# A smaller leading tile for the first convolution of a speech joint network, with its weight sums on other operands and engines

## The chip, the cores and the metric

One core of a Trainium2 chip. The metric is the device time of one execution in microseconds (us), as the median of several runs. Engines: TensorE (PE; its weight loads are the row PEld), VectorE (DVE), ScalarE (ACT), GpSimd (POOL) and SyncE (SP), which issues nearly all DMAs.

## The reference

Two strided convolutions over time, then a joint network. All tensors are bf16.

```python
B, T, D, K, U = 2, 4000, 512, 5, 8
h = sum over i of einsum("btc,cd->btd", xp[:, i:i+T, :], w1[i])      # xp: x padded by 2 at both ends
h = gelu(h)[:, ::2, :]                                              # 2000 rows per batch element
f = sum over i of einsum("btc,cd->btd", hp[:, i:i+T1, :], w2[i])
f = gelu(f)[:, ::2, :]                                              # 1000 rows
fe = einsum("btd,de->bte", f, w_f);  ge = einsum("bud,de->bue", g, w_g)
j = tanh(fe[:, :, None, :] + ge[:, None, :, :])
out = einsum("btud,dv->btuv", j, w_o)                               # 2 x 1000 x 8 x 512
```

## The kernel before, in words

**Tiles.** Channels stand on the 128 partitions, in four blocks of 128; time runs along the free dimension. The first convolution (conv1) of batch element 0 is cut into three tiles: a leading one of 2 x `NA` = 408 outputs, and two later ones with `N3` = 266 columns each, which give 3 x 266 = 798 outputs each (L311). Batch element 1 is two tiles of 334 columns, and the second convolution (conv2) two tiles of 334.

**The leading tile** is computed plainly. Its rows of x are loaded as they stand (`load_xr`, two loads of 128 and 78 rows of four time steps), turned on TensorE against an identity (`turn`, L489), and copied from PSUM into `xs`. Then `direct` (L691) runs 80 matmuls, 5 taps by 4 by 4 blocks, in the order of taps 0, 4, 2, 1, 3, each with 408 moving columns, into four PSUM banks.

**A later tile** (`Triple`, L562, and `Unit`, L607) computes three neighbouring outputs together from nine products, each on sums and differences of inputs and of weights. Its inputs come by transposing DMAs, one for each of six phases of time (`xq`, `load_xq`, L464). The sums of inputs are made in 17 `STEPS` (L773): "d" copies a doubled phase, "r" and the rest subtract or add, "next" and "prev" copy a shifted phase. A product is 16 matmuls (4 by 4 blocks), a tile 9 x 16 = 144. For each output block, `Unit` runs five steps with copies out of PSUM between them: `s1` keeps 1.5 times the first product ("c"), `s2` keeps minus the next ("s"), `s3` to `s5` finish the three outputs.

**The sums of conv1's weights** (`w1part`, L542) are made on the chip, block by block of 128 output channels (m = 0 to 3), on 512 elements per partition: t = w0 + w4, u = 4 w4 + w0, u = 2 w2 + u, v = t - w2, and t + w2, all on VectorE in SBUF; ScalarE then writes u/3 and v/3 as bf16 into `w1_x`. w1 + w3, w1 - w3 and 2 w1 are made for two blocks at a time. The first products of a later tile need u/3 of all four blocks and the first difference of x.

**The order.** Every operation is recorded with its reads and writes (`Plan`, L110). `ORDER`, a table of characters at the head of the file, holds for each engine the list of recorded operations in the order in which it runs them. The kernel holds the finished table, not what made it. `schedule` (L199) reads it; `flex` (L130) records an operation that can run on either of two engines, and the table then says on which. `emit` places the waits that the order leaves needed. So an engine never passes over an operation that waits.

**PSUM.** Banks 0 to 3 hold the leading tile; banks 4 to 7 and then 3 go to the units of the later tiles.

**After the convolutions** the features and the joint output are computed by fast (seven-product) block multiplications, whose sums are on VectorE or GpSimd, tanh on ScalarE, evictions on ScalarE and VectorE, and stores on SyncE's queue.

Of the kernel before, what the change touches and what calls it, by code (L numbers as in the profile page):

```python
# [12 lines left out]
P = 128  # L13
# [50 lines left out]
class Op:  # L64
# [6 lines left out]
        "0Y0Z0a0b0c0d0e0f0g0i0k0l0n0q0y0z0_0-101112131415161718191A1B1C1D1E1F1G1H1p2L2l321I1J2v2S2T1r1s2w2n2N2o2O34352y2V2z2W"  # L71
        "3F3G3C3D392s3X2t3A3Y3Q3S3g3T403a3b3q4A3n3i3r3j3d4J423e4T4B434U3o473t4L4j4M4D3u484E4h4W4Q4k4R5U4X4u4r4x4s4o524z4p4_4v"
        "5e55565y535f586667595W5X5b5c6U5_6W5h6e6X5-6f6u6h6i6364695i6-726b6c6w6A736x707H7a7J7K7y7R7k7O7l7S7h7U7P757V7i7c867d7_"
        "7-767n8c8C897o8A8M87838N8J848e8K8f8E8F8v8_8w8m8n989990918j8P958k8Q9B8x8y9M9O8p9P8q9T9U969Z9a9c9C9o9x9d9W9z9X9qA5ACA2"
        "ABA4A99sAWAGAI9tArAsANAKB3B4BAAiAQAjATBBARAUBMAlAmBeBNAoApBfBtAyAzBGBhBiA-BTBUB0BDBHBEBJCABzBaBKBbBWBXCBBkBlCQCHB_CI"
        "CNBnC0COC1BqBoCKBrCLCuCcC6CdCRCfCvCgCTCjCkC7CxCyCUDODSDBDCDTC_DeDEC-DFCnCoD1DVD2DWDfDYDKDZDlDoDLDpDmDwE1E2D4E4E5D5Db"
        "DcDxDsDtENE7E8EOEKEDEEEiEAEjEBELEcEXEYEdF7ETEoFLEUF0EfElFMEgF1F8FXEmFDFOFfF3FBFPFgFsF4F_G4F-FRFiG5FZFjFSFUFVG1G2GNGG"
        "GHGTGUFoFpFuGAGWG7G8GZGXGJGKGOGaGnGoGcGqGrGhGfHCGwGxH0GdHEH3H1HVH4H9HWHAHbHhH6I4I5HKHNHcHLH7HOHjHpHqHeHYHZHfHRHSIAI7"
        "I8IKHyHzHsIhIbIBILHtIcIiIDJ4J5INIOIRIeISIEIkJKIrIsIfJAJBIlJLJDI_J7IuIvJXI-J8JdJaJbJYJEJgJeJRJNJhK0K1JnJoJSJqJwJOKGK6"
        "JrK3K4KHKbJxK7KVKWK9KcKAKYKZL0KeKfKlKmKNL1KOKJKuL6KKKoL7LZKpL3LTL9KvLGLULaLHLALcL4LyLNLsLjLOLkLtLzLdLJLKLWM2LXM3MCMR"  # L80
        "L-M0MSMuMDMvLmLnM5MJM6MhMiMKMFMUMXMGMVMYMaMxMyMbM_N1M-NPN8N9MoMkNQMpN2MlNBNCNFNGNSNTNYNuNvO1ONNZOONfNgNiNjNVNWN_O2Nx"
        "NyN-O8OdNmOeNnO9OwOTOWOUOxOqOrOXOBOQOCOtOROFOkOuOGP4OzP5OgPBPCOlOhP7O_PHPIPKP8PLPiQ9PjPQPRPNPOQAPXPYPaPrPoPpPbPsPlPm"
        "PyPePfPzQMP-Q0Q3Q4QNQCQDQIQJQFQGQPQQQTQUQXQYQbQeQfQi"),
    "act": (
        "080h0m1U0r1x1W1a1z1Z251Y2b1q271K2m1L2M1-1j2U1t2x1l1M1O332d2R1N3E2g2f2X2u2_3Z3B3H3R2h3h413c2r3K3s3M4K3x3f4C4V3p3y3w38"
        "494F4b3m3W3v4i5V5D464t4Y4P4S4y4d5C574q4w5z5B4n6E5A5g5154685d6V6g786j6v6G6M6a5j65795S6B5a745T627I7A7b6d7s5x7z7T717N6_"
        "7W7j7m5q6T7Q5w778D8d7u7g828O8B886s6t7p6S8X8-8L858o8Y9A8W9G8I8R8i8l9N7G948r9I976m9b9V9D9e9S8z9p9_9rA69YAcAXA8AFAtAdAP"
        "AfAMAeAhASAnBOAVB8BuB9AgBgCFCECs9wB7CGCqB-CJC2CCCrCDCeCwChDQCtDPDRFJDDD-CpE0DGDgEaDnFHCXEbE3D6FxFFFGFID_FwEMEFEZEPGS"
        "FyEpFNF2FYFKG_FCF5FhFzIWFkG-GIGVFvI0IVJ2GpGRGgGsHDJVH2J_HXI2IYHMHPI6I1IXIaJ-IMICIjJ6IdJ3ItI3IZJMIwJWJZK_JfK2JpKTJsNN"
        "KILSKdKRK-KnL2KUKyKqLwL8LVLILRLlL_NqKSLxM4MTMEMwMtMjMHKzMQNsN0MPMmNDNLNRMsOPNhNwNXNkNtNMOfOMNOODNrOpP6OLOiPJOoP9PPPZ"  # L90
        "PkQBPcPqP_Q1QOQHQRQgQdQk"),
    "dve": (
        "000j0o0p1R1S1v1T1V1X231w1u212Z1_1y24221b2a261d1c1Q1e1g1f1P1h1i1k28202p1m2P2Y362c1n2Q2q372e1o302i2k2j2-3U3I3V313J3L3k"
# [191 lines left out]
def bass_standalone__seq2seq_rnn_t_joint__speech_kernel(  # L285
# [35 lines left out]
    with ExitStack() as es:  # L321
# [142 lines left out]
        def load_xq(i, ph):  # L464
            o = load_x6(xq[i], 0, ph, 2 * NA // 3 + i * N3[0] - 2, 0, -(-(N3[i] + 3 - i) // 16) * 16)
            if (i, ph) in ((0, 4), (0, 0)):
                o.wire = 1.050 if ph else 2.520
# [768 lines left out]
```

## Time and profile before

| what | value |
|---|---|
| runs | 248.55, 249.01, 249.67 us (median 249.01) |
| profiled execution, first to last instruction (span) | 247.2 us |
| TensorE busy | 242.8 us, 98% |
| VectorE busy | 224.8 us, 91% |
| ScalarE busy | 210.7 us, 85% |
| GpSimd busy | 83.8 us, 34% |

The profile gives the span of its execution; the execution's own total time is not listed beside it, so the median of the runs stands for it, 1.8 us above the span. The profile's page has busy times, 40 slices of the span, the chain that ended last, and groups of instructions by line of the kernel. Other views of the same trace list instructions in order of time, by tile, by stage and by wait. A row of the view in order of time reads: start, length from first start to last end, engine, line, operation, what it writes and reads with sizes, count, and the idle time ahead of it with what ended it. Neighbouring instructions on an engine overlap a little, so distances between starts, not lengths, add up to a queue's time.

### The profile page before, as it was taken

What the parts mean: (1) busy time and instruction counts of PE and PEld (TensorE: products, weight loads), DVE (VectorE), ACT (ScalarE), POOL (GpSimd) and SP (SyncE); (2) the same over time, 40 slices, a digit from 0 to 9 for tenths busy, and PEclk for the clock granted to TensorE, in tenths of its full rate; (3) what the DMA queues carried; (4) which work ended last, traced back from release to release, by engine and by line L of the source; (5) the groups of instructions that cost most, each with busy time, mean ns of one, the idle gap of its engine ahead of it and who ended that gap; (6) DMA issues with size and microseconds to landing.
All of it is one profiled execution on the core that took longest, in us unless ns stands there. A gap on an engine that the chain in (4) does not pass through costs nothing.

```text
span 247.2 us, 5277 instructions
## 1 busy us (share of the span) xinstructions
PE 242.8 (98%) x1932; PEld 186.1 (75%) x1932; DVE 224.8 (91%) x403; ACT 210.7 (85%) x359; POOL 83.8 (34%) x90
## 2 busy tenths in 40 slices
PE   8999999999999999999999999999999999999995
PEld 4657888877666666666567888778788888888883
DVE  1799998867999999699998999999999999999994
ACT  3269799899669857986799999999999999999992
POOL 1000000000000000000015584677887886796861
PEclk9999999999999999999999999999999999999999
DMA  6998999997700340000000234413433655356377
GB/s 215 331 193 168 185 157 205 150 177 174 254 2 3 119 135 3 1 1 3 0 0 3 85 102 139 143 48 129 131 127 103 195 171 172 132 187 200 123 258 233
DMA packets 57890, 31.87 MB, mean 129 GB/s; under 512 B 33835, under 2 KB 57659, under 8 KB 57865
## 3 DMA queue, kind: packets, MB, share of 16 engines
q1 hardware_dynamic: 57577, 31.41, 48.5%
q8 instruction: 15, 0.25, 0.4%
q10 hardware_dynamic: 288, 0.13, 0.2%
q14 instruction: 10, 0.08, 0.1%
HBM read 7.66 MB, written 16.38 MB: 97 GB/s over the span
## 4 chain that ended last, share of the span: by engine, by line
PE 98%; DVE 0%; issue 0%
PE acc L412 97%; PE acc L496 1%; DVE ost L835 0%; DVE xs L505 0%; DVE zero L419 0%
## 5 line engine op out<-in xcount | busy, mean ns | idle before, releaser
L398 DVE TENSOR_TENSOR og<-acc,sn 128x512 bf16<-128x512 f32 x93 | 60.0, 690 | 1.9 <-PE acc L412 1.2
L412 PE MATMUL acc<-tw,ss 128*128 128x256 f16 x372 | 58.0, 273 | 0.0
L404 ACT ACTIVATE jT<-feT,geT 128x1000 bf16<-128x1000 f32 (+6 forms) x56 | 53.2, 1002 | 1.8 <-DVE feT L398 1.5
L834 ACT ACTIVATE sn<-acc 128x512 f32<-128x512 f32 (+1 forms) x70 | 43.0, 707 | 1.0 <-PE acc L412 0.7
L412 PEld LDWEIGHTS acc<-tw,ss 128*128 128x128 f16 x372 | 36.0, 98 | 6.5 <-ACT sn L834 0.2
L903 POOL TENSOR_TENSOR ss<-jT 128x512 f16<-128x512 bf16 x24 | 27.7, 1168 | 25.0 <-DVE feT L398 22.5
L412 PE MATMUL acc<-row,w_sb 128*128 128x334 bf16 (+1 forms) x192 | 31.7, 296 | 0.0
L412 PE MATMUL acc<-wo_sb,jT 128*128 128x256 bf16 x176 | 29.2, 273 | 0.0
L404 ACT ACTIVATE sd<-acc 128x334 f32<-128x334 f32 (+1 forms) x48 | 20.6, 435 | 10.1 <-PE acc L412 9.6
L412 PE MATMUL acc<-row,w_x 128*128 128x266 bf16 (+1 forms) x192 | 28.4, 291 | 0.0
L404 ACT ACTIVATE jX<-feT,geT 128x1000 bf16<-128x1000 f32 (+4 forms) x28 | 27.4, 1042 | 0.0
L394 POOL MEMSET hT<- 128x8 bf16 (+2 forms) x6 | 0.7, 149 | 70.5 <-ACT hT L404 70.5
L412 PEld LDWEIGHTS acc<-row,w_sb 128*128 128x128 bf16 x192 | 18.7, 98 | 6.3
L412 PEld LDWEIGHTS acc<-row,w_x 128*128 128x128 bf16 x192 | 18.7, 98 | 5.7
L903 POOL TENSOR_TENSOR ss<-jT,ss 128x512 f16<-128x512 bf16 x14 | 16.6, 1189 | 15.1 <-DVE ss L903 9.7
L412 PE MATMUL acc<-wo_sb,ss 128*128 128x256 bf16 x124 | 21.0, 273 | 0.0
L412 PEld LDWEIGHTS acc<-wo_sb,jT 128*128 128x128 bf16 x176 | 17.2, 98 | 3.1
L835 DVE COPY sn<-acc 128x512 f32<-128x512 f32 (+1 forms) x25 | 16.8, 691 | 1.1 <-PE acc L412 1.0
L412 PE MATMUL acc<-hT,w_sb 128*128 128x334 bf16 x96 | 17.1, 305 | 0.0
L518 DVE SCALAR_TENSOR_TENSOR acc<-acc,sd 128x334 f32<-128x334 f32 (+1 forms) x24 | 11.7, 487 | 5.8 <-PE acc L412 5.6
L404 ACT ACTIVATE hT<-acc 128x266 bf16<-128x266 f32 (+2 forms) x36 | 14.6, 433 | 2.7 <-PE acc L412 2.4
L834 ACT ACTIVATE og<-acc 128x512 bf16<-128x512 f32 x22 | 15.3, 710 | 1.5 <-PE acc L412 1.5
(113 smaller groups left out, 502.5 us busy)
## 6 DMA issues: line engine op xcount, KB each, us to landing
out_dram<-og SPq DMA_DIRECT2D x45, 256.0 KB, 2.3
w_sb<-in_w_dram SPq DMA_DIRECT2D x8, 512.0 KB, 4.9
out_dram<-og SPq DMA_DIRECT2D x19, 128.0 KB, 2.2
w_sb<-in_w_dram SPq DMA_DIRECT2D x4, 256.0 KB, 4.8
xr<-in_x_dram SPq DMA_DIRECT2D x1, 512.0 KB, 3.5
wf_sb<-in_w_f_dram SPq DMA_DIRECT2D x1, 512.0 KB, 3.6
wg_sb<-in_w_g_dram SPq DMA_DIRECT2D x1, 512.0 KB, 5.1
wo_sb<-in_w_o_dram SPq DMA_DIRECT2D x1, 512.0 KB, 5.2
```

The lines of the kernel that those rows point to most:

```text
L394: pl.op("pool", lambda e: e.memset(v.ap, 0.0), (), (v,))
L398: pl.op(eng, lambda e: e.tensor_tensor(out=o.ap, in0=a.ap, in1=b.ap, op=op), (a, b), (o,), 0.02 + 2.14e-3 * o.ap.free_size() if eng == "po ...
L404: pl.op("act", lambda e: e.activation(o.ap, i.ap, func, scale=scale, bias=0.0 if bias is None else bias.ap), rd, (o,), o.ap.free_size() * ...
L412: ins = e.matmul(o.ap, lhsT=l.ap, rhs=r.ap, start=start and n == 0, stop=stop and n == len(pairs) - 1, skip_group_check=not check)
L496: ins = e.transpose(pv.ap[:, i, k, :], xr[rt].h[0:n, 2 * r + pp, k, :], ident.h[0:n, 0:n])
L518: pl.op(eng, lambda e: e.scalar_tensor_tensor(out=o.ap, in0=a.ap, scalar=f, in1=b.ap, op0=ALU.mult, op1=add), (a, b), (o,), vec_cost(o, (a ...
L834: pl.flex({"act": (lambda e: e.activation(o.ap, v.ap, ACT.Copy), 0.05 + n * 0.833e-3), "dve": (lambda e: e.tensor_copy(out=o.ap, in_=v.ap) ...
L835: "dve": (lambda e: e.tensor_copy(out=o.ap, in_=v.ap), 0.065 + n * 1.04e-3)}, (v,), (o,))
L903: fn = lambda e, o=S[i], x=x, y=y, op=op: e.tensor_tensor(out=o.ap, in0=x.ap, in1=y.ap, op=op)
```

## The change

The leading tile goes from 408 to 360 outputs and the two later ones from 266 and 266 to 234 and 314 columns; the buffers of the transposed loads grow with it.

```diff
-        NA, N3 = 204, (266, 266)
+        NA, N3 = 180, (234, 314)
-        xq = [Buf(nc, f"xq{i}", [6, NK, (288, 288)[i]], BF16, v.end - v.bytes) ...]
+        xq = [Buf(nc, f"xq{i}", [6, NK, (352, 352)[i]], BF16, v.end - v.bytes) ...]
```

The loads of taps 1 and 3 are gated by an earlier arrival: tap 3 waits for the first half of tap 4 instead of the second.

```diff
-                              (4, (slice(0, NK), slice(D // 2, D)), 0), (2, None, 1), (1, None, 3), (3, None, 5)):
+                              (4, (slice(0, NK), slice(D // 2, D)), 0), (2, None, 1)):
             load_w1(i, part, gate)
-        for ph in (4, 0, 2, 1, 3, 5):
-            load_xq(0, ph)
+        for kind, i in (('w', 1), ('w', 3), ('x', 4), ('x', 0), ('x', 2), ('x', 1), ('x', 3), ('x', 5)):
+            if kind == "w":
+                load_w1(i, None, len(came) - 4)
+            else:
+                load_xq(0, i)
```

The weight sums: for every block, ScalarE first copies tap 4 into a PSUM bank (of banks 4 to 7), and u is built there. For blocks 0 and 1 ("P") t and v are in PSUM too, on VectorE. For blocks 2 and 3 ("G") GpSimd makes t, v and t + w2 in SBUF. The sums of taps 1 and 3 may run on either engine.

```diff
+        WBANK = ((6, 7), (5, 4), (6, 7), (5, 4))
+        WHOME = ('P', 'P', 'G', 'G')
...
+            home = WHOME[m]
+            if home != "S":
+                u, t = (ps.cols(bk * NT, NT).map(lambda a: a.rearrange("p (k c) -> p k c", k=NK)) for bk in WBANK[m])
+                act(u, w(4), ACT.Copy)
+                w4 = u
...
+            if home == "G":
+                t, v = ssum[4][:], ssum[m % 2][:]
+                tt("pool", t, w(0), w(4), add)
+                tt("pool", v, t, w(2), sub)
+                tt("pool", w1_t[2, :, sl], t, w(2), add)
+            else:
+                v = t if home == "P" else ssum[m % 2][:]
+                tt("dve", t, w4, w(0), add)
+            stt("dve", u, w4, 4.0, w(0))
+            stt("dve", u, w(2), 2.0, u)
+            act(w1_x[1, :, sl], u, ACT.Copy, scale=1.0 / 3.0)
+            if home != "G":
+                tt("dve", w1_t[2, :, sl], t, w(2), add)
                 tt("dve", v, t, w(2), sub)
+            act(w1_x[0, :, sl], v, ACT.Copy, scale=1.0 / 3.0)
+
+        def w13part(m):
+            n = slice(m * P, (m + 2) * P)
+            shared(w1_x[2, :, n], w1_sb[1, :, n], w1_sb[3, :, n], sub, True)
+            shared(w1_t[0, :, n], w1_sb[1, :, n], w1_sb[3, :, n], add, True)
+            scaled(w1_t[1, :, n], w1_sb[1, :, n], 2.0)
```

The scaled copies of `Triple` and `Unit` (steps "d", "next", "prev", and "c" and "s") go through `scaled`, which lets the table put them on ScalarE or VectorE.

```diff
+        def scaled(o, i, f):
+            n = o.ap.free_size()
+            fast = not i.psum and o.ap.dtype == BF16 and i.ap.dtype == BF16
+            pl.port = fast
+            pl.flex({"act": (lambda e: e.activation(o.ap, i.ap, ACT.Copy, scale=f), n * 0.833e-3 + (0.05 if i.psum else 0.105)),
+                     "dve": (lambda e: e.tensor_scalar_mul(out=o.ap, in0=i.ap, scalar1=f), 0.065 + n * (0.26e-3 if fast else 1.04e-3))}, (i,), (o,))
+            pl.port = False
...
-                    act(r(i, n=E), z(2 * i - 2, 0, E) if i else z(4, -1, E), ACT.Copy, scale=2.0)
+                    scaled(r(i, n=E), z(2 * i - 2, 0, E) if i else z(4, -1, E), 2.0)
...
-                act(self.c, self.pa(), ACT.Copy, scale=1.5)
+                scaled(self.c, self.pa(), 1.5)
```

The zeroed edges of the second tile's input are written phase by phase (six small writes on GpSimd, not two). The planner's figures for the turns change (0.275 to 0.43, 0.2 to 0.19), and the whole `ORDER` table is replaced: every engine's order is new, from the start of conv1 to the last store. In it ScalarE's second copy of turned rows comes before the weight sums, 18 of the scaled copies are on VectorE, GpSimd has 77 of the two-operand sums of the later stages instead of 71, and at the end the product for the last two-operand eviction stands behind the first half of the last plain tile, not ahead of it.

More of the change, by code (lines that the diff above doesn't have):

```diff
@@ L780, in steps @@
             when(slot, *[lambda w=w: trip[i].step(w) for w in STEPS[lo:hi]])
-        w1part(0, "s")
+        for m in range(NK):
+            w1part(m, "s")
+        for m in (0, 2):
+            w13part(m)
         for w in STEPS:
             trip[0].step(w)
-        for m in range(1, NK):
-            when((0, 0, 1)[m - 1], lambda m=m: w1part(m, "s"))
         when(17, load_late, lambda: tail_zero(1))
```

108 lines of the change are left out of this document (48 added, 60 removed).

## The prediction

> **What bounds the kernel now.** I read the page first, then the chain that ended last, the waits of TensorE, and the opening 30 us engine by engine.
>
> ```profile
> PE 242.8 (98%) x1932; PEld 186.1 (75%) x1932; DVE 224.8 (91%) x403; ACT 210.7 (85%) x359; POOL 83.8 (34%) x90
> PE   8999999999999999999999999999999999999995
> PEclk9999999999999999999999999999999999999999
> ```
>
> TensorE is busy in every slice at a full granted clock. The chain that ended last (start, length, what) and the waits of TensorE agree:
>
> ```profile
> 4.78 2.18 PE acc L496 x24
> 6.96 0.02 issue
> 6.99 0.33 DVE xs L505
> 7.32 0.05 issue
> 7.37 236.76 PE acc L412 x1892
> ...
> 244.15 0.42 DVE ost L835
> ```
> ```profile
> PE acc L412 <- DVE zero L419: 1.2, 1, 1.2
> ```
>
> From 7.37 to 244.15 us the chain never leaves TensorE, and its only listed wait is the one before its first instruction. So the time is an opening of 7.37 us, a stream of matmuls without gaps, and a tail. Only the columns streamed, the opening and the tail can shorten it; any wait added between lengthens it. A busy TensorE could hide small gaps, so I look at the starts:
>
> ```profile
> 4.58 2.66 PE L496 MATMUL acc<-ident,xr 128*128 128x128 bf16 x32
> 7.37 12.65 PE L412 MATMUL acc<-xs,w_sb 128*128 128x408 bf16 x72
> 19.86 1.98 PE L412 MATMUL acc<-row,w_x 128*128 128x266 bf16 x16
> 21.67 1.54 PE L412 MATMUL acc<-xs,w_sb 128*128 128x408 bf16 x8
> ```
>
> Start to start, a 408-column matmul takes (19.86 - 7.37)/72 = 173.5 ns and a 266-column one (21.67 - 19.86)/16 = 113.1 ns: 0.425 ns per column more, with nothing left for a gap.
>
> The span of this execution is 247.2 us; the median of the runs is 249.01, so 1.8 us lie around the span. I change the span and keep the 1.8.
>
> **The change part by part. Columns.** The 80 leading matmuls go from 408 to 360 columns: 80 x 48 x 0.425 = -1.63 us. The first later tile has 144 matmuls (9 products, 4 by 4 blocks) at 234 columns, not 266: 144 x 32 x 0.425 = -1.96. The second has 144 at 314: 144 x 48 x 0.425 = +2.94. Sum **-0.65 us**.
>
> This needs the spacing to go on falling down to 234 columns, though each matmul has its own weight load. The nearest narrow row has 16 columns:
>
> ```profile
> 108.49 0.35 PE L412 MATMUL acc<-gT,wg_sb 128*128 128x16 bf16 x8
> 108.69 0.73 PE L412 MATMUL acc<-row,w_t 128*128 128x334 bf16 x4
> ```
>
> Eight matmuls with eight weight loads pass in 0.20 us, 25 ns each, so weight loads set no floor near 99 ns here. The Trainium skill (TensorE: Matmul & The Clock Gate, LDWEIGHTS) gives P/1.2 ns for a load of P columns, 107 ns for 128, an estimate above the 99.5 ns of a 234-column matmul; by it the sum would be about 1 us longer. The row of 25 ns speaks against it; it is rival D.
>
> **Opening.** TensorE may start the leading tile when the second set of turns (16 transposes, now 54 rows each, not 78) has been copied out.
>
> ```profile
> L496 PE MATMUL acc<-ident,xr 128*128 128x128 bf16 x16 | 1.9, 314 | 0.0
> L496 PE MATMUL acc<-ident,xr 78*128 78x78 bf16 x16 | 0.9, 228 | 0.0
> 5.67 0.42 DVE L505 COPY xs<-acc 128x512 bf16<-128x512 bf16 x1 [4.54 <-PE acc L496]
> 6.99 0.92 DVE L505 COPY xs<-acc 128x312 bf16<-128x312 bf16 x2 [0.89 <-PE acc L496]
> ```
>
> The 24 turns of the chain took 2.18 us, though the wide ones alone, by the starts, 16 x 0.107 = 1.71 with 0.20 of it before the chain picks them up: the eight narrow ones that VectorE waits for took 2.18 - 1.51 = 0.67, or 0.08 each at most. At 54/78 of that I save up to 0.2; the copy shrinks from 312 to 216 elements, (0.42 - 0.33)/200 x 96 = 0.04. I take **-0.2 us** (bounds 0 and -0.25). The leading tile then starts at 7.17 and its first 72 matmuls, 153.1 ns each, end at **18.2**, not 19.86. Everything the first later tile needs is due 1.66 us sooner.
>
> **Is it there at 18.2?** In the new order the sums of conv1's weights start with a ScalarE copy of tap 4 into PSUM, then 14 VectorE passes of 512 elements (blocks 0 and 1 whole, of blocks 2 and 3 the 4:1 sums), then the first difference of x; ScalarE's scaled copies free the four PSUM banks which the first products then write: a wait that was not there. The prices:
>
> ```profile
> 7.99 0.69 DVE L398 TENSOR_TENSOR ssum<-w_sb 128x512 f32<-128x512 bf16 x1
> 11.38 0.69 DVE L398 TENSOR_TENSOR ssum<-ssum,w_sb 128x512 f32<-128x512 f32 x1
> 11.98 0.69 DVE L398 TENSOR_TENSOR w_t<-ssum,w_sb 128x512 bf16<-128x512 f32 x1
> 18.00 0.72 DVE L398 TENSOR_TENSOR row<-xq 128x1064 bf16<-128x1064 bf16 x1
> 27.33 0.44 DVE L518 SCALAR_TENSOR_TENSOR acc<-acc,sd 128x266 f32<-128x266 f32 x1
> 27.68 0.71 DVE L398 TENSOR_TENSOR row<-row 128x1064 bf16<-128x1064 bf16 x1
> ```
> ```profile
> 11.50 0.63 ACT L404 ACTIVATE w_x<-ssum 128x512 bf16<-128x512 f32 x1 [4.28 <-DVE ssum L518]
> 12.03 0.67 ACT L404 ACTIVATE xs<-acc 128x624 bf16<-128x624 bf16 x1
> ```
>
> A pass of 512 takes 0.60 us from start to start. With PSUM in and out, 266 elements took 0.35, so 512 at about 1 ns each come to 0.60 too: the PSUM operand is no faster and no slower (bounds 0.60 and the displayed 0.69). Tap 4 is there at 8.0, where before's first sum starts; the copy takes 0.53 (not shown into PSUM; bounds 0.45 and 0.7). 8.5 + 14 x 0.60 = 16.9, the difference of 936 elements 0.55: **17.5**. ScalarE's two last copies for the first product follow pass 13: 16.3 + 2 x 0.53 = **17.4**. Both lie 0.7 us ahead of 18.2. That is the cover; beyond it each further 0.1 us is paid by TensorE.
>
> The transposed loads of x have no wait before the 18.00 row above, and are smaller ahead of it (240 rows, not 272; second load of x 54 rows, not 78), so I cost them at nothing. Those of the second tile grow to 320, but its VectorE work starts 4 us after its first load is due.
>
> **GpSimd** takes over, early, seven passes' worth of 512: three for block 2, two for block 3 and one of 1024; block 3's third comes later, behind waits for the second tile's loads, and has 2 us and more to spare.
>
> ```profile
> L903 POOL TENSOR_TENSOR ss<-jT 128x512 f16<-128x512 bf16 x24 | 27.7, 1168 | 25.0 <-DVE feT L398 22.5 <-PE acc L412 2.4
> L1009 POOL TENSOR_TENSOR fs<-fs,wf_sb 128x512 f16<-128x512 f16 x1 | 1.3, 1269 | 2.6 <-DVE fs L1009 2.6
> 1.68 2.94 SPq L458 DMA_DIRECT2D w_sb<-in_w_dram  x4
> w_sb<-in_w_dram SPq DMA_DIRECT2D x4, 256.0 KB, 4.8
> 10.77 0.69 DVE L518 SCALAR_TENSOR_TENSOR ssum<-w_sb,ssum 128x512 f32<-128x512 bf16 x1 [0.88 <-DMA w_sb<-in_w_dram]
> ```
>
> The second half of tap 4 is issued by 4.6 and lands near 9.0; tap 2 is there at 10.7. At 1.17 us a pass, 512 by 512: first pass done 10.2, second 11.9, the 1024 one 16.6, the next 17.8. ScalarE reads the second near 14.9. TensorE needs the 1024 one near 22.6 (18.2, then 28 matmuls of 99.5 ns and 8 of 153, then 4 more). The last feeds a ScalarE copy that must start by 22.4, since the copies behind it let TensorE go on at 23.4. Cost nothing; float32 operands are not shown on GpSimd, so the bounds are 1.17 and twice that (rival B).
>
> **Copies.** Eighteen copies of the two convolutions move from ScalarE to VectorE: twelve within SBUF of 936 to 1344 elements and six of 314 or 334 out of PSUM. A plain SBUF copy on VectorE is not shown; the nearest row, two operands of 1064, takes 0.62. At that they cost VectorE 12 x 0.7 + 6 x 0.4 = 11 us over 17 to 120 us, less the 4.2 us (seven passes) that it sheds early.
>
> ```profile
> 20.00:30.00 10.00, 10.00 (x87) 8.16 (x85) 9.99 (x18) 8.50 (x17) 0.22 (x2) 1.00 0.96 176
> 50.00:60.00 10.00, 10.00 (x81) 7.64 (x80) 6.44 (x12) 8.89 (x18) 0.00 (x0) 1.00 0.83 158
> 60.00:80.00 20.00, 20.00 (x144) 13.84 (x142) 19.93 (x33) 15.43 (x31) 0.17 (x1) 1.00 0.31 103
> 100.00:120.00 20.00, 20.00 (x150) 13.20 (x149) 17.52 (x33) 16.54 (x31) 0.17 (x1) 1.00 0.01 2
> ```
>
> The third pair in each row is VectorE. Each instruction shows about 0.09 us (0.69 - 0.60) that overlaps the next, so 33 in 19.93 us occupy 17, and 12 in 6.44 occupy 5.4: which leaves 4.6, 3.0 and 5.5 us in the last three rows alone, 13 for 11 less 4.2. Cost nothing; without that cover TensorE would pay the excess, some tenths a stage.
>
> **Tail.** In the new order the product that feeds the last two-operand eviction comes after four matmuls of 109 ns, not before them, so its store is issued 0.44 us later and the last one on the same queue after it.
>
> ```profile
> 243.04 1.67 SPq L959 DMA_DIRECT2D out_dram<-og  x3
> 243.71 0.60 ACT L834 ACTIVATE og<-acc 128x512 bf16<-128x512 f32 x1 [1.24 <-PE acc L412]
> ```
>
> That queue's last issue ended at 244.71, starting as ScalarE's eviction ended. The later store's issue, some 0.4 us long, now runs 244.08 to 244.48, so the last begins 0.15 us later: **+0.15 us** (bounds 0 and +0.44).
>
> The sum: -0.65 - 0.2 + 0.15 = -0.7 us; the span 246.5, the time 247.2 - 0.7 + 1.8 = **248.3 us**.
>
> **Rivals.**
>
> **A, the sums are late (20%).** VectorE's chain to 17.5 has 0.7 us of cover. At 0.69 a pass with PSUM at both ends it is 14 x 0.09 = 1.26 later, TensorE waits 0.55 at 18.2, and the gain is given back: the change does not do what it says. 248.85; with a little more at the next products, 249.0. For it: VectorE at 9.99 of 10 us in the 20 to 30 row. Against: the 0.35 us between the two last VectorE rows above.
>
> **B, slower: GpSimd (10%).** Were a pass 2.4 us with float32 operands or beside VectorE's own SBUF reads, the seven end at 9.0 + 7 x 2.4 = 25.8. The last feeds a ScalarE copy that stands ahead of the three that release the banks: TensorE, due 23.4, gets its first at 25.8 + 0.53 + 0.3 = 26.6 and waits 3.2. 248.3 + 3.2 = **251.5**. It decides from (22.4 - 9.0)/7 = 1.9 us a pass; at 2.0 the gain is gone. Against: the 24 passes of the row above ran at a mean of 1.17 us while VectorE was as busy.
>
> **C, the first GpSimd pass is slow (4%).** If it took 6 us more, the second ends near 18, ScalarE's queue behind it reaches the first product's bank near 19.5 to 20.5, and TensorE waits 1.3 to 2.3: about 250.0. Before's first such pass shows nothing of it:
>
> ```profile
> 125.64 1.15 POOL L903 TENSOR_TENSOR ss<-jT 128x512 f16<-128x512 bf16 x1 [22.51 <-DVE feT L398]
> ```
>
> It took 1.15, and its idle time is put down to VectorE alone; but a load before it would have lain in that idle time. The Trainium skill (GPSIMD Engine Reference, Instruction dispatch) says the first call to freshly loaded code pays some 6 us that no profile instruction shows; by that rule this case would hold if these passes count as such, which no run here shows.
>
> **D, a floor under the 234-column matmuls (3%).** At 107 ns they cost 144 x 7.5 = 1.1 us more: 249.4.
>
> **E, the new order also drops what little waiting the stream and the ends still hold (13%).** With no cost at the tail, the full 0.25 at the start and another 0.3: 248.3 - 0.5 = 247.8, at best 247.5.
>
> **How the numbers follow.** The forecast has 50%: 248.3, its own range 247.9 to 248.7 from the bounds of opening and tail. A 20, E 13, B 10, C 4, D 3. Leaving out B and the lowest edge of E, the range is **247.6 to 250.0**. About 0.5% (1.25 us) is what a measurement of this kernel can tell from no change. Faster by over that is below 247.76: half of E and a sliver of the forecast, 10%. Slower is above 250.25: B, a part of C, and 2 of A where more than one wait follows: 14%. Within: 76%.
>
> **What would show it.** Right: matmuls of 360 columns 153 ns apart, of 234 near 99.5; the first 234-column product starting near 18.2 with no wait of TensorE between 7.2 and 243; GpSimd passes near 1.2 us. Wrong: TensorE waiting on ScalarE or VectorE between 18 and 24 us (A, B or C, told apart by whether VectorE's passes, GpSimd's, or only its first are long), spacing above 105 ns at 234 columns (D), or VectorE without any gap from 30 to 100 us and TensorE waiting for it there, which I cost at nothing.

## The result and the profile after

The changed kernel takes **249.32 us** (median of 22 runs, 248.62 to 249.88); the kernel before took 248.76 us beside it (22 runs, 248.43 to 249.67). The ratio is 1.002, with a 95% interval of 1.0012 to 1.0027: 0.56 us slower, where 0.7 us faster was forecast. The profiled execution has a span of 247.8 us (its time 249.59), 0.64 us more than before's 247.16 (shown as 247.2).

The page of the changed kernel first: the span, the engines, and TensorE's slices.

```profile
span 247.8 us, 5298 instructions
PE 240.9 (97%) x1932; PEld 185.1 (75%) x1932; DVE 229.3 (93%) x408; ACT 196.8 (79%) x345; POOL 100.1 (40%) x107
PE   7999999999999999999999999999999999999993
PEclk9999999999999999999999999999999999999998
```

TensorE has 1.9 us less to do and the span is longer all the same. The slices do not show where: a wait of half a microsecond is a tenth of a slice. The waits of TensorE and the order of its work do.

```profile
PE acc L412 <- DVE acc L521: 0.6, 1, 0.6
PE acc L412 <- DVE row L398: 0.4, 1, 0.4
PE acc L412 <- ACT hT L404: 0.3, 1, 0.3
```
```profile
4.21 1.06 PE L499 MATMUL acc<-ident,xr 128*128 128x128 bf16 x16
5.48 0.57 PE L499 MATMUL acc<-ident,xr 54*128 54x54 bf16 x16 [0.22 <-DMA xr<-in_x_dram]
6.37 11.20 PE L412 MATMUL acc<-xs,w_sb 128*128 128x360 bf16 x72 [0.32 <-DVE xs L508]
18.01 1.77 PE L412 MATMUL acc<-row,w_x 128*128 128x234 bf16 x16 [0.44 <-DVE row L398]
...
21.32 2.56 PE L412 MATMUL acc<-row,w_x 128*128 128x234 bf16 x24 [0.32 <-ACT hT L404]
23.72 2.56 PE L412 MATMUL acc<-xq,w_t 128*128 128x234 bf16 x24
26.12 0.96 PE L412 MATMUL acc<-row,w_x 128*128 128x234 bf16 x8
26.92 0.56 PE L412 MATMUL acc<-row,w_sb 128*128 128x234 bf16 x4
28.09 0.97 PE L412 MATMUL acc<-row,w_sb 128*128 128x234 bf16 x8 [0.61 <-DVE acc L521]
```

Twenty-four matmuls of 234 columns pass from 23.72 to 26.12, 100 ns each, as forecast. But the stream has three holes, each measured from the start of the last matmul ahead of it to the start of the next, less the spacing of one matmul: 0.61 us ahead of 18.01, 0.49 ahead of 21.32, 0.78 ahead of 28.09. Before had none above 0.13 in its stream. (The idle time in brackets is shorter than the hole, since a matmul's shown end lies past its share of the stream.)

From before to after, the spans differ by 247.80 - 247.16 = +0.64 us, and the two traces put it so: the leading tile starts at 6.37, not 7.37 (-1.0); 1536 columns fewer (-0.64); the three holes less 0.13 of a small one in before (+1.74); other small gaps (-0.26); from TensorE's last matmul to the end of the span 3.84 us, not 3.05 (+0.79). Their sum is 0.63. In the chains of both kernels the last lines give that end: 247.2 - 244.13 before, and here 247.8 - 243.97.

```profile
28.09 215.88 PE acc L412 x1736
243.97 0.02 issue
244.00 0.42 DVE ost L869
```

### The profile page after: what moved, and what is told of

It reads as the page before. It is cut to its first block, busy times and chain, and to the rows that moved or that the text cites. A ratio compares the mean times of both kernels' runs of the same rounds, so it can differ in the third digit from the quotient of the medians.

```text
span 247.8 us, 5298 instructions
## 1 busy us (share of the span) xinstructions
PE 240.9 (97%) x1932; PEld 185.1 (75%) x1932; DVE 229.3 (93%) x408; ACT 196.8 (79%) x345; POOL 100.1 (40%) x107
## 4 chain that ended last, share of the span: by engine, by line
PE 89%; ACT 4%; DVE 3%; DMA 2%; SPq 1%; issue 0%; ACTq 0%
PE acc L412 89%; DMA w_sb<-in_w_dram 2%; ACT w_x L404 2%; DVE acc L521 1%; DVE row L398 1%; ACT acc L404 1%; ACT row L550 1%; ACT w_t L550 0%; SPq L458 0%; SPq L438 0%; ACT sd L550 0%; DVE w_t L398 0%; DVE acc L398 0%; DVE ost L869 0%; ACT hT L404 0%
## 5 line engine op out<-in xcount | busy, mean ns | idle before, releaser
L404 ACT ACTIVATE jT<-feT,geT 128x1000 bf16<-128x1000 f32 (+6 forms) x56 | 51.3, 980 | 0.0
L412 PE MATMUL acc<-row,w_sb 128*128 128x334 bf16 (+2 forms) x192 | 32.6, 297 | 0.6 <-DVE acc L521 0.6
L550 ACT ACTIVATE sd<-acc 128x334 f32<-128x334 f32 (+2 forms) x42 | 17.7, 432 | 19.1 <-PE acc L412 18.8
L412 PE MATMUL acc<-row,w_x 128*128 128x334 bf16 (+2 forms) x192 | 29.2, 292 | 0.8 <-DVE row L398 0.4
L404 ACT ACTIVATE jX<-feT,geT 128x1000 bf16<-128x1000 f32 (+4 forms) x28 | 25.9, 944 | 0.0
L404 ACT ACTIVATE hT<-acc 128x334 bf16<-128x334 f32 (+3 forms) x36 | 14.5, 435 | 8.1 <-PE acc L412 8.0
L412 PEld LDWEIGHTS acc<-wo_sb,jT 128*128 128x128 bf16 x176 | 17.2, 98 | 2.5
L937 POOL TENSOR_TENSOR ss<-jX 128x512 f16<-128x512 bf16 x14 | 16.2, 1173 | 2.5 <-ACT jX L404 1.9
L937 POOL TENSOR_TENSOR ss<-jT,ss 128x512 f16<-128x512 bf16 x11 | 13.3, 1216 | 8.6 <-DVE ss L937 8.6
L869 DVE COPY sn<-acc 128x512 f32<-128x512 f32 x25 | 16.6, 684 | 0.1
L412 PE MATMUL acc<-xp,w_t 128*128 128x334 bf16 x96 | 16.5, 304 | 0.0
```

Of the source, the lines that this page charges most:

```text
L404: pl.op("act", lambda e: e.activation(o.ap, i.ap, func, scale=scale, bias=0.0 if bias is None else bias.ap), rd, (o,), o.ap.free_size() * ...
L412: ins = e.matmul(o.ap, lhsT=l.ap, rhs=r.ap, start=start and n == 0, stop=stop and n == len(pairs) - 1, skip_group_check=not check)
L550: pl.flex({"act": (lambda e: e.activation(o.ap, i.ap, ACT.Copy, scale=f), n * 0.833e-3 + (0.05 if i.psum else 0.105)), "dve": (lambda e: e ...
L869: "dve": (lambda e: e.tensor_copy(out=o.ap, in_=v.ap), 0.065 + n * 1.04e-3)}, (v,), (o,))
L937: fn = lambda e, o=S[i], x=x, y=y, op=op: e.tensor_tensor(out=o.ap, in0=x.ap, in1=y.ap, op=op)
```

## The experiments

Each ratio is to the kernel before on the same chip (median 248.8 to 248.9). Differences to the changed kernel compare medians that were taken on different chips, so some tenths of a microsecond between them say little; the traces decide. `ORDER` names an operation by two characters; an edit of it is shown as the changed stretch of one engine. The tokens are those of the changed kernel.

**The third hole: who waits for whom.** VectorE and GpSimd of the changed kernel around 26 us:

```profile
25.73 1.48 POOL L398 TENSOR_TENSOR w_t<-ssum,w_sb 128x512 bf16<-128x512 f32 x1
```
```profile
25.55 0.65 DVE L398 TENSOR_TENSOR row<-row 128x936 bf16<-128x936 bf16 x1
26.11 1.60 DVE L398 TENSOR_TENSOR row<-row,xq 128x936 bf16<-128x936 bf16 x1
27.64 0.40 DVE L521 SCALAR_TENSOR_TENSOR acc<-acc,sd 128x234 f32<-128x234 f32 x1
```

The same kind of subtraction takes 0.65 us in one row and 1.60 in the next, and GpSimd's pass, block 3's third, takes 1.48 and not 1.16. The two overlap: GpSimd's pass ends at 27.21, and 0.5 us later VectorE's subtraction does; GpSimd itself was 0.3 us late, the rest of the subtraction begun at 25.55. VectorE's next operation evicts the bank that TensorE waits for. The theory: with both operands in SBUF, VectorE and GpSimd do not work at the same time. The first experiment moves the pass behind GpSimd's next small write, which has a load of x to wait for; nothing else.

```diff
-"pool": 0w 0x 1t 0y
+"pool": 0w 0x 0y 1t
```

> The changed kernel with GpSimd's last sum for conv1's block 3 (the 512-element pass that ran from 25.73 to 27.21 us) moved one place back in GpSimd's queue, behind the next small write, which waits for the second tile's third load (27.05 us). Theory 1, the block: that GpSimd pass held up VectorE's subtraction of two SBUF operands which started at 26.11 and took 1.60 us instead of 0.65, and so the wait of TensorE of 0.78 us at 27.2. Moved, it falls beside VectorE operations with one PSUM operand; the subtraction is back near 0.65 us, that wait of TensorE is gone, and the time falls by 0.6 to 0.8 us, from 249.3 to about 248.6. Rival 1, VectorE's queue was late anyway: the subtraction may get shorter, TensorE still waits 0.4 us or more there, and the time falls by less than 0.3 us.

Measured: 248.84 us (12 runs), ratio 1.0002 (0.9991 to 1.0013), 0.48 us less than the changed kernel (whose interval, 1.0012 to 1.0027, just touches this one). The pass now starts at 27.00, when VectorE works on PSUM operands, and both take their usual time:

```profile
27.00 1.16 POOL L398 TENSOR_TENSOR w_t<-ssum,w_sb 128x512 bf16<-128x512 f32 x1
```
```profile
25.89 0.64 DVE L398 TENSOR_TENSOR row<-row,xq 128x936 bf16<-128x936 bf16 x1
26.44 0.40 DVE L521 SCALAR_TENSOR_TENSOR acc<-acc,sd 128x234 f32<-128x234 f32 x1
```

The hole at 27 us is gone. The block itself only moved: the pass, which ends at 28.16, now meets VectorE's next operation on two SBUF operands, and that one takes 1.02 us from 27.81 on, where it took 0.80 in the changed kernel. TensorE needs neither result yet. (In three later expectations this edit is worded the wrong way round: the pass goes behind the small write, not ahead of it.) The reverse test gives GpSimd more: one more sum, of two SBUF tiles, right where VectorE makes the row differences.

```diff
-"dve": ... 20 ...     (w1 + w3 of blocks 2 and 3)
+"pool": 1s 20
```

> The changed kernel with one more sum of conv1's weights on GpSimd: the pass of 1024 elements out of two SBUF tiles that VectorE runs near 18.1 us (0.68 shown, 0.6 a step) is run by GpSimd from 17.4 us on. Theory (GpSimd and VectorE block each other while VectorE has two operands in SBUF): GpSimd takes up to 2.13 us there, and VectorE's row differences, all of two SBUF operands, stand still meanwhile; the row difference for the second product is ready 1.3 to 1.5 us later although VectorE has 0.6 us less to do, and TensorE's wait near 20.7 us grows from 0.49 to about 1.9: 250.4 to 250.9. Rival (the engines run independently): VectorE is 0.6 us sooner, the wait near 20.7 us goes, 248.8 to 248.9.

Measured: 251.34 us (4 runs), ratio 1.0108 (1.0086 to 1.013), 2.0 us above the changed kernel. (The sum that moved is VectorE's at 24.36 us and not, as the expectation says, the one near 18.1; so VectorE is relieved only after 20.7 us, and the rival's gain could not have come there.) The hole at 21 us is 2.43 us, not the 1.9 expected. In order, GpSimd and VectorE of this kernel, and the row of the changed kernel for VectorE's copy:

```profile
17.55 2.62 POOL L588 TENSOR_TENSOR w_t<-w_sb 128x1024 bf16<-128x1024 bf16 x1
```
```profile
17.55 0.64 DVE L398 TENSOR_TENSOR row<-xq 128x936 bf16<-128x936 bf16 x1
18.10 2.40 DVE L551 TENSOR_SCALAR row<-xq 128x944 bf16<-128x944 bf16 x1
```
```profile
17.82 0.39 DVE L551 TENSOR_SCALAR row<-xq 128x944 bf16<-128x944 bf16 x1
```

GpSimd starts together with a subtraction, waits for it (2.62 us, against 2.13 for a pass of that size at 14 us in the changed kernel), and then VectorE stands still for the whole pass: a copy of 0.39 us takes 2.40. That copy has one operand. So the theory was too narrow: the bf16 copy from SBUF to SBUF blocks as well, and that is why more was lost than expected. The Trainium skill (SBUF — State Buffer, Who interferes with whom) states this rule: VectorE and GpSimd share one pair of SBUF ports as an exclusive lock, VectorE takes it with two SBUF inputs or in its 2-port modes, which a `tensor_scalar` can enter, and the order of issue decides who blocks. The two rows of 1.60 and 2.40 us agree with it. The diff had it in sight: `pl.port` marks just these operations.

**Is it always so?** A kernel that differs only at the end (below) had no hole between 17 and 28 us in its profiled execution, whose leading tile started at 7.15:

```profile
26.06 1.39 POOL L398 TENSOR_TENSOR w_t<-ssum,w_sb 128x512 bf16<-128x512 f32 x1
```
```profile
25.79 0.64 DVE L398 TENSOR_TENSOR row<-row,xq 128x936 bf16<-128x936 bf16 x1
26.35 0.40 DVE L521 SCALAR_TENSOR_TENSOR acc<-acc,sd 128x234 f32<-128x234 f32 x1
```

Here the last subtraction had begun first, GpSimd waited for it, and nothing was lost. The pass begins after a small write that waits for a load of x, and its place against VectorE's work moves from execution to execution by some tenths of a microsecond. That fits the spread of the times (248.62 to 249.88), but single executions were not matched with theirs. Leaving one_more_sum aside, seven profiled executions have the smaller tile, the new orders and the pass in its place. In five of them a VectorE subtraction takes 1.57 to 1.61 us and the holes behind it add up to 0.72 to 1.01 us; in the other two all subtractions take 0.64 or 0.65 and there is no hole. The five executions that moved the pass have none above 0.2 us there.

**The first two holes.** In the changed kernel VectorE's first row difference starts at 17.21 and takes 0.68; the product waits for it. The second hole ends right after a second row difference (20.52, 0.65). One edit takes that one sooner (it also swaps 2B and 29 behind it):

```diff
-"dve": 23 1y 2A 27 26 28 2B 29 1z
+"dve": 23 2A 27 26 28 1y 29 2B 1z
```

> The changed kernel with one VectorE operation (the 1024-element difference of taps 1 and 3 for blocks 0 and 1) moved four places back, behind the difference that the second product of the first later tile needs. Theory 3, VectorE's queue sets the second product: its input is ready 0.6 us sooner, near 20.5 us, and TensorE's wait of 0.49 us at 20.7 us is gone or below 0.1 us; the time falls by up to 0.5 us if nothing behind it is late, and by about 0.1 us if the block of theory 1 (VectorE's 1.60 us operation) takes it back at 27 us: then the wait there grows to about 1.2 us. Rival 3, what the profile names as the releaser there, ScalarE's gelu of the leading tile: the wait of 0.49 us stays.

Measured: 249.29 us (10 runs), ratio 1.0025 (1.0015 to 1.0035): no gain. The holes at 17 and 20 us are gone in its profile, though its leading tile started late, at 6.97, which closes the first by itself. The second was closed by the edit: the first product starts at 18.00 as in the changed kernel (18.01), so the second falls due at the same time. The third grew to 1.01 us (VectorE's subtraction again 1.60, GpSimd's pass 1.60). What was gained ahead of the block was lost in it. Leaving one_more_sum aside, the second hole (0.43 to 0.54 us) stands in six of the seven executions that have the smaller tile and the new orders without this edit, and in none of the five with it.

**The end, first theory.** The forecast put +0.15 us on the order of the last operations. Undone:

```diff
-"pe":  Qj Qf Qg Qm Qn Qq      "dve": Qd Qk Qh Qr      "act": QZ Ql Qo Qs
+"pe":  Qf Qg Qj Qm Qn Qq      "dve": Qd Qh Qk Qr      "act": QZ Qo Ql Qs
```

> The changed kernel with only the last six operations of TensorE and the matching last evictions of VectorE and ScalarE put back in the order of the kernel before (the product for the last two-operand eviction ahead of the first half of the last plain tile). In the traces the time from TensorE's last matmul to the end of the span was 3.0 us before and 3.8 us after. Theory 2, the order: the stores then stand less densely in SyncE's queue, the last is issued 0.3 us sooner and the span's end comes 0.4 to 0.7 us sooner; the time falls to about 248.8. Rival 2, the stores simply land with that much scatter: no change beyond 0.15 us, and the distance from the last matmul to the end stays between 3.0 and 3.8 us whatever the order. My prediction's own price for this step was 0.15 us.

Measured: 249.4 us (10 runs), ratio 1.0027 (1.0017 to 1.0036), and the end is 3.85 us, as in the changed kernel. The theory falls: these six operations do not set the end. They were the only ones that the forecast had looked at.

**All three edits**, and one swap on VectorE ("2H 3E" to "3E 2H").

> The three edits together, and VectorE's first step of block 2's last sum put ahead of the blocked subtraction. If the three theories hold, TensorE waits only at the first product of the first later tile (0.6 us or less, depending on how early the leading tile starts), and the time is 249.3 - 0.7 - 0.4 - 0.4, about 247.8 us, 0.4% under the kernel before. If the rivals hold, 249.0 us or more.

Measured: 248.45 us (12 runs), ratio 0.9996 (0.9984 to 1.0008): 0.87 us less than the changed kernel by the medians, 0.6 by the ratios. It is 0.65 above what was expected; 0.4 of that had been put on the end, which stayed at 3.83. Its chain:

```profile
6.62 11.19 PE acc L412 x72
17.81 0.12 issue
17.93 7.79 PE acc L412 x72
25.72 0.04 issue
25.76 217.07 PE acc L412 x1748
```

TensorE never leaves the chain after 6.62 us. In this trace the second hole is gone, in that of the first experiment it is 0.44 us. What the sooner row difference is worth in time is not shown: the median is 0.39 us below the first experiment, but by the ratios it is 0.15, and the two intervals overlap.

**Size alone and order alone.** The kernel before with the smaller tile only, and the changed kernel with the old sizes.

```diff
-NA, N3 = 204, (266, 266)    xq (288, 288)
+NA, N3 = 180, (234, 314)    xq (288, 320)     # in the kernel before
```

> The kernel before with one part of the change alone: the leading tile has 360 outputs, the later ones 234 and 314; the order of before, its sums on VectorE out of SBUF and its copies are kept. The columns are worth -0.65 us and the opening 0 to -0.25. If the sums are late (theory: the smaller tile needs the new sums), TensorE ends the leading 72 matmuls near 18.0 to 18.2, while before's first row difference is ready near 18.7 and its scaled copies near 19.1 and 20.0: waits of 0.5 to 1.3 us, so the gain is spent and the time is 248.5 to 249.5. Rival: nothing is late, no wait of TensorE between 17 and 30 us, 248.0.

Measured: 251.9 us (4 runs), ratio 1.0122 (1.0104 to 1.014), outside both expectations: +3.1 us. The end is 3.03 us. The holes add up to 3.5 us: 0.89 and 0.50 at 18 and 20 us as reckoned, small ones to 28 us, and 1.33 at 33.7 us, which I had not seen. There the row difference of the second later tile comes late:

```profile
34.03 0.12 POOL L394 MEMSET xq<- 128x32 bf16 x1 [2.44 <-DMA xq<-in_x_dram]
34.19 0.81 DVE L398 TENSOR_TENSOR row<-xq 128x1256 bf16<-128x1256 bf16 x1 [1.02 <-POOL xq L394]
```

It waits for GpSimd's write of the zeroed edges, which in the kernel before covers two phases at once and so waits for the last load of this tile (33.99, in before 32.04). The changed kernel writes them phase by phase. Whether the larger loads or the joint write cost the time was not separated. So the smaller tile needs the rest of the change, which buys back some 2.6 us.

```diff
-NA, N3 = 180, (234, 314)
+NA, N3 = 204, (266, 266)     # in the changed kernel
```

> The changed kernel with the tile sizes of before (408, 266, 266): the new sums, copies and orders without the smaller leading tile. Theory: the leading matmuls now end 1.6 us later than in the changed kernel, so its waits at 17 and 20 us (0.61 and 0.49) are gone; the wait of 0.78 us behind GpSimd's late pass stays if that pass still meets a VectorE operation on two SBUF tiles; the tail stays 0.75 us longer than before's. Against the kernel before that makes +0.8 +0.75 = up to +1.5 without any gain by columns: 249.7 to 250.4. Rival: what costs the time is the smaller tile itself (sums due sooner): then this kernel is level with before, 248.9.

Measured: 249.36 us (12 runs), ratio 1.0019 (1.0007 to 1.0031). That lies between the two expectations. The three holes are gone: the first product falls due some 2.5 us later (19.91, not 17.40), the sums are there in time, and GpSimd's late pass (26.11 to 27.27) meets an idle VectorE. TensorE's last matmul comes at 244.03 (before 244.11), and the end is 3.96 us. That single difference is the loss: the new order's end costs 0.5 to 0.9 us, whatever the tile.

**The end, second theory.** SyncE's stores in the last 9 us (start, length from first to last, count), before and after:

```profile
238.46 1.93 SPq L951 DMA_DIRECT2D out_dram<-og  x3
240.55 1.26 SPq L849 DMA_DIRECT2D out_dram<-og  x3
241.85 0.39 SPq L959 DMA_DIRECT2D out_dram<-og  x1
242.50 0.39 SPq L951 DMA_DIRECT2D out_dram<-og  x1
```
```profile
239.38 1.73 SPq L985 DMA_DIRECT2D out_dram<-og  x3
241.15 1.40 SPq L883 DMA_DIRECT2D out_dram<-og  x3
242.59 0.39 SPq L993 DMA_DIRECT2D out_dram<-og  x1
243.03 0.47 SPq L985 DMA_DIRECT2D out_dram<-og  x1
243.54 1.59 SPq L993 DMA_DIRECT2D out_dram<-og  x3
```

The last row of before is in the prediction (243.04, 1.67, x3). Before's queue has a gap ahead of nearly every store, and its last three take 1.67 us because the last of them waits for ScalarE. After, from 240.2 us on, each store begins as the one ahead ends; the last three take 1.59 us in one piece, and the queue ends 1.17 us after TensorE's last matmul (before 0.60). The first stores of the row begin late, because the products that fill them end later in TensorE's new order. Og0's store, the first row, is issued 243.96 - 239.38 = 4.58 us ahead of the last matmul's end, 5.65 in before. Seven experiments move these stores or lighten the load. First one store:

```diff
-"pe": Pm Pi QU Pj Q7 Pn     "dve": P- Po
+"pe": Pm Pn Pi QU Pj Q7     "dve": Po P-
```

> The changed kernel with one edit at the end: the product that closes the bank of og1's second quarter is moved four TensorE operations sooner, and VectorE evicts it ahead of og2's first quarter, as in before, so that the first store of og1 can be issued 0.6 us sooner. Theory (the end is SyncE's queue of ten stores, back to back at 0.4 to 0.5 us each, which begins late): the whole queue moves forward, and from TensorE's last matmul to the end of the span it takes 3.2 to 3.5 us, not 3.84; time -0.35 to -0.6, 248.75 to 248.95. Rival (the end is set by the last eviction and its store, whatever stands ahead of it): 3.8 us, 249.3.

Measured: 249.27 us (12 runs), ratio 1.0014 (1.0 to 1.0029); end 3.99 us. The first store of og1 came 3.93 us ahead of the last matmul's end and not 3.78, a quarter of what was meant: in the same queue the store of og0 ahead of it waited for a ScalarE eviction, and came 0.22 us later than in the changed kernel (4.36, not 4.58). The same edit on top of all_three:

> The changed kernel with all edits so far: GpSimd's late sum ahead of the pass that it stood behind, the row difference for the second product sooner on VectorE, the last six TensorE operations as in before, and og1's store sooner. If the gains add up (all but the tail gave 248.45 against 248.89 for the kernel before), this is 248.45 - 0.45 = 248.0, 0.9 us faster than before, near what was forecast for the change. Rival: the tail does not move, 248.45.

Measured: 248.83 us (12 runs), ratio 1.0003 (0.9991 to 1.0015), end 4.0 us. No gain. Then the store ahead as well:

```diff
-"pe": QH Px Q4 QI Pt Q5 Pu PZ Pm Pi QU Pj Q7 Pn     "act": QJ Q6 Py Pk
+"pe": QH Px Pi Pj Q4 QI Pt Q5 Pu PZ Pm Pn QU Q7     "act": QJ Pk Q6 Py
```

> The changed kernel with the ends of two products moved sooner. In the run before this one only the second of the late stores was moved, but the store of og0 ahead of it in SyncE's queue waited for ScalarE's eviction at 5.2 us before TensorE's end, so nothing could move. Here the product of that og0 eviction ends eight TensorE operations sooner and ScalarE evicts it ahead of two copies, and og1's second quarter goes as in the run before. Theory (a queue of stores that moves bytes at a full rate to the end, and begins late): og0's store is issued near 5.8 us and og1's near 4.4 us before TensorE's last matmul, and from that matmul to the end of the span it takes 3.2 to 3.4 us, not 3.84. Rival (the end does not depend on these stores): 3.8 us. Time by the theory 248.75 to 248.95 against 249.3; 0.5 us is near what the spread of the opening hides, so the distance in the profile decides.

Measured: 249.99 us (5 runs), ratio 1.0042 (1.0028 to 1.0055). The end is 3.49 us, so these stores bear on it; but TensorE waits 0.51 us at 237.0, because the product continues in a bank that VectorE has still to read. Slower on balance.

> The changed kernel with GpSimd's late sum ahead of the pass that it stood behind, the row difference for the second product sooner, the last six TensorE operations as in before, and both stores sooner. If the gains add, 248.45 to 248.8 (the two sets so far) less 0.45: 248.0 to 248.3, 0.5 to 0.9 us faster than the kernel before. Rival: the distance from the last matmul to the end stays 3.8 us, 248.45 to 248.8.

Measured: 249.37 us (11 runs), ratio 1.0021 (1.0011 to 1.003): the same hole of 0.51 us, end 3.47. With that product three operations later:

```diff
-"pe": QH Px Q4 QI Pt Q5 Pu PZ Pm Pi QU Pj Q7 Pn
+"pe": QH Px Q4 QI Pt Pi Pj Q5 Pu PZ Pm Pn QU Q7
```

> The changed kernel with the two products at the end moved sooner as in the run before, but the one into the bank that VectorE still had to read is put three TensorE operations later, so that TensorE does not wait for it (it waited 0.51 us there). Theory: og0's store is issued near 5.2 us and og1's near 4.3 us before the last matmul, no wait of TensorE after 200 us, end 3.4 to 3.5 us after the last matmul: -0.35 us against the changed kernel, 248.95. Rival: the end follows the bytes, not these two stores, and stays at 3.8 us: 249.3.

Measured: 249.24 us (12 runs), ratio 1.0008 (0.9995 to 1.0021). No wait of TensorE after 200 us, and the end is 3.48 us, as the theory had it:

```profile
241.32 1.23 SPq L883 DMA_DIRECT2D out_dram<-og  x3
242.59 0.39 SPq L993 DMA_DIRECT2D out_dram<-og  x1
243.21 0.39 SPq L985 DMA_DIRECT2D out_dram<-og  x1
243.65 1.55 SPq L993 DMA_DIRECT2D out_dram<-og  x3
```

The 0.36 us are in the profile; in the times they do not show beyond the spread. This execution also has a hole of 1.22 us at 17.6, which has nothing to do with its end:

```profile
18.14 0.65 DVE L398 TENSOR_TENSOR row<-xq 128x936 bf16<-128x936 bf16 x1 [0.92 <-DMA xq<-in_x_dram]
```

VectorE stood ready for the first row difference at 17.2, as in the changed kernel, and waited for a transposed load of x that landed at 18.11; in the changed kernel the same load landed at 16.65.

> The same end together with GpSimd's late sum ahead of the pass that it stood behind, the row difference for the second product sooner, and the last six TensorE operations as in before. If the gains add: 248.45 (the same without this end) - 0.35 = 248.1, 0.75 us faster than the kernel before. Rival: no gain at the end, 248.45 to 248.8.

Measured: 248.82 us (12 runs), ratio 0.9998 (0.9988 to 1.0008), end 3.5 us; 248.1 was expected. In no version did the gain at the end show in the median. Last, whether earlier bytes hold up the last stores:

```diff
+few = len(jts) - 5 <= self.n < len(jts) - 3
-e.dma_start(dst, src.ap)
+e.dma_start(dst[0:8], src.ap[0:8]) if few else e.dma_start(dst, src.ap)
```

> The changed kernel with five earlier stores cut: of the fifth and the fourth tile from the end, each store writes 8 rows and not all of its rows, so most of the output of these two tiles is left out. Instructions, their order and their waits stay. Theory (the DMA engines, busy at 1.0 of their time in the last 6 us, still move the bytes of these earlier stores and hold up the last ten): with about 1 MB less to move, the ten last issues take 0.38 us each and not 0.5, the last is issued as soon as ScalarE's last eviction ends (0.3 us after the last matmul, not 0.68), and the end of the span comes 3.0 to 3.2 us after the last matmul, not 3.84. Rival (ten issues in a row take 0.5 us each, whatever the bytes): 3.8 us.

Measured: 249.33 us (10 runs), ratio 1.0012 (0.9998 to 1.0027), end 3.80 us; the last stores run as in the changed kernel.

The theory of the earlier bytes falls: with almost nothing of the earlier stores to move (they are six, not five, 1.0 MB in all), the last ten issues take the same 0.37 to 0.57 us. Five of the six cut stores were themselves issued in 0.28 to 0.30 us, 0.39 to 0.60 in the changed kernel, so the length of an issue goes with what that store itself writes.

The bytes of the last stores are another matter. Here is what the DMA engines did from the last matmul to the end of the span, before, changed, tail_third and few_stores (the last two figures are the busy share and GB/s):

```profile
244.11:247.16 3.05, 0.00 (x1) 0.00 (x0) 0.42 (x1) 0.20 (x1) 0.00 (x0) 1.00 0.64 183
243.96:247.80 3.84, 0.00 (x0) 0.00 (x0) 0.42 (x1) 0.28 (x1) 0.00 (x0) 0.79 0.72 215
244.30:247.78 3.48, 0.00 (x1) 0.00 (x0) 0.42 (x1) 0.28 (x1) 0.00 (x0) 0.80 0.72 214
243.78:247.57 3.79, 0.00 (x0) 0.00 (x0) 0.42 (x1) 0.28 (x1) 0.00 (x0) 1.00 0.73 217
```

Rate times length gives 0.56, 0.83, 0.74 and 0.82 MB still to move when TensorE stops: the longer the end, the more of the output is left. Stores that are issued late leave more bytes for the end, and the cut of few_stores took away bytes that had already landed. Bytes and lateness of the last stores were not varied apart from each other.

## Why the prediction was wrong

**In short.** The sum put TensorE's waits at nothing, and they came to 1.74 us: 0.78 behind a GpSimd pass that was costed at nothing, 1.10 behind sums and row differences that came later than due, less 0.13 of a small wait that before had. The tail was 0.79 us, not 0.15. The columns were right. The time moved the other way than forecast, and that it still lies inside the stated range of 247.6 to 250.0 is luck: an opening 0.8 us sooner than forecast, which is not shown to be the change's doing, hid part of these misses in the profiled execution.

**Columns: right.** -0.65 us forecast, 1536 columns fewer found, matmuls 153 and 100 ns apart. Rival D, a floor near 107 ns, is refuted by the row of 23.72; so is the estimate that was drawn from the Trainium skill's figure for weight loads (TensorE: Matmul & The Clock Gate, LDWEIGHTS).

**Opening: right in sign, but not shown to be the change's.** The start of the leading tile lay between 6.34 and 7.38 us in 14 profiled executions with 54 narrow rows, and at 7.37 and 7.42 in the two with 78. The wide turns are spaced 107 ns at first and 56 later, and the switch came anywhere between 3.8 and 6.9 us. In the changed kernel all 16 wide turns came after it (1.06 us in the row above), in before none did (1.71). In three of the 14 the profile puts the idle time ahead of the leading tile down to a load of weights instead. The -0.2 us cannot be separated from these. And a start at 6.37 makes the first product due at 17.40, ahead of the 18.2 that I forecast.

**"Is it there at 18.2?" missed by 0.4 us.** The fourteen passes took 0.60 us each as forecast, but began at 8.84 and not 8.5: tap 4 landed at 8.12, not 8.0, ScalarE's copy into PSUM began 0.09 later, and it took 0.60 to its end, not 0.53. The first row difference ended at 17.89, against 17.5 forecast, and let TensorE go at 18.01. The 0.7 us of cover was spent by a late chain and an early stream. Rival A is what happened here, in part: the two first holes, 1.10 us in this execution. Its reason, slower passes with PSUM operands, is not what happened. The place of the second hole, a row difference that the second product needs, is in no step of mine.

**GpSimd: the step that failed.** I wrote of block 3's third pass that it "has 2 us and more to spare" and cost nothing. Its own result had time: in the first experiment it was done 0.95 us later, and nothing waited for it. What I left out is that the pass holds up another engine: VectorE's subtraction took 1.60 us instead of 0.65, and TensorE waited 0.78. Taking the pass away from there gave back 0.48 us in the median; giving GpSimd one more pass, of 1024 elements, cost 2.0. Rivals B and C went past it too: they asked how long a pass takes, and found the right answer (1.15 to 1.17 us with float32, and the first began 0.07 us after its load landed at 8.97 and was no slower), but not whom it stops. The argument against B, that 24 passes had run at 1.17 us beside a busy VectorE, said nothing about VectorE's side.

**Transposed loads: not free.** I costed them at nothing because VectorE never waited for one in before. There the load in question landed 0.95 us ahead of its use (17.05 and 18.00); in the changed kernel 0.56 us (16.65 and 17.21), and in tail_third, with the same opening, 0.9 us too late, which cost TensorE the hole of 1.22 us. That is one of 13 executions with the new orders and the smaller tile. In size_alone a wait of 1.33 us hung on the second tile's last load and the edge write behind it.

**Copies: no cost shown.** The plain copy of 944 elements took 0.39 us where I allowed 0.7; no stage from 30 to 230 us has a wait of TensorE. The 18 copies were not moved back by themselves.

**Tail: right in sign, mis-sized.** +0.15 us with bounds 0 and 0.44 was forecast, +0.79 measured, and it is no scatter: the end took 3.80 to 3.96 us in the eight executions that keep the late products of the changed kernel, and 3.02 to 3.05 in the two with the order of before. I priced one store and one eviction. But the whole order of TensorE's last stage had changed: the products that the first of the last stores wait for closed later, the ten last stores, 0.5 us apart, outlast the last eviction, and 0.83 MB instead of 0.56 were left to move. Moving two products took 0.36 of it back; the other 0.43 was not traced to single operations.

The forecast's span was 246.5, the measured one 247.8: +1.3, of which the tail is 0.64, the holes 1.74, the opening -0.8 and other small gaps -0.26 (rival E had allowed 0.3 for these). No version measured beats the kernel before: the best, 248.45, lies at 0.9996 with an interval that holds 1.

## What to carry to other kernels

Before work is given to an idle engine "with time to spare", list which operations of the other engines cannot run beside it; for GpSimd these were here VectorE's with two SBUF operands and its bf16 copy from SBUF to SBUF, and the cost is VectorE's delay, not GpSimd's. Where a stage is moved sooner, compare the earliest start of the stream with the latest end of the chain, and with the latest landing of its loads, over several executions, since each moves by itself. When the order of the last stage is new, count the stores and the bytes that are queued at the end, not the last store alone.

## What the runs showed of the hardware

- GpSimd and VectorE block each other in whole instructions: 0.64 to 1.61 us for a subtraction of two SBUF operands, 0.39 to 2.40 for a bf16 copy from SBUF to SBUF, and GpSimd's own passes 1.16 to 1.60 and 2.13 to 2.62. With an operand in PSUM VectorE ran beside GpSimd at its usual 0.60 us a pass from 9 to 17 us.
- The first matmuls run at half speed (107 ns for 128 columns, then 56). The switch came between 3.8 and 6.9 us after the start, while the granted clock in the profile reads 1.00 in every window of 2 us from 0 to 8 us, before and after: 1 us of difference between executions of the same opening. The Trainium skill (TensorE: Matmul & The Clock Gate, Part 1: The HAM clock gate) explains it by a window of 3.4 us that runs freely, and says that the point varies by 0.5 us either way; here it varied over 3.1 us.
- A store's issue takes 0.37 to 0.39 us on SyncE when it stands alone (the last 6 us of before), up to 0.57 when ten follow each other, also with 1 MB less written just before, and 0.28 to 0.30 us for a store cut to 8 of its rows.
- Behind the last matmul the end of the span went with the output still to move: 3.05 us with 0.56 MB, 3.48 with 0.74, 3.84 with 0.83.
